# A scan followed by a mixture of adapters on one core: ScalarE copies the transposed weights as 32-bit words, early filler matmuls are halved, and the written-out orders of all engines are replaced

## The chip, the cores and the metric

The kernel runs on one core of a Trainium2 chip. A core has five instruction streams that run side by side and meet only at semaphores: TensorE (PE, with its weight loads as PEld), VectorE (DVE), ScalarE (ACT), GpSimd (POOL) and SyncE (SP), which here only issues transfers between device memory and on-chip memory. The metric is the time of one execution on the device in microseconds (us), as the median of several runs. Before the change it is 201.59 us (three runs, 201.13 to 202.28).

## What is computed

The inputs are `a` and `b`, each 8 x 6400 x 128 in float32. For each of the 8 sequences a linear recurrence runs along the 6400 steps, for 128 channels by themselves. Its 51200 rows x then go through eight small adapters of rank 16, of which each row takes the two with the highest gate logits:

```
h = a[:, t] * h + b[:, t];  x[:, t] = h          # the scan, 6400 steps
logits = x @ w_gate                              # 51200 x 8
top two of the 8 logits, softmax over the two -> weights w
out = x + sum over the two of  w * ((x @ A[e]) @ B[e])
```

## The kernel before

**Tiles.** The 51200 rows are cut into 100 chunks of 512 rows, 4 blocks of 128 rows each. Loads and stores take two chunks at a time (512 KB for `a`, 512 KB for `b`, 512 KB for the result); the first four chunks and the last four stores are single (256 KB). `NL = 6` buffers of two chunks hold each of `a` and `b`; the result waits in a ring of 72 blocks (18 chunks). Two chunks share a load so that the lower 64 partitions hold the first and the upper 64 the second.

**Stages of a chunk c**, with the names that the written-out orders use:

- `la`, `lb` (SP): loads. The very first `lb0` is issued by ACT, as are the three small weight loads `ca`, `cw`, `cb`.
- `A`, `B` (PE): transposes of `a` and `b` into PSUM, channels on partitions; `P{c}` does B of chunk c and A of chunk c+1 in alternation, 16 matmuls.
- `ae` (ACT): copy of the transposed `a` from PSUM to `a_st`, 128x512 float32.
- `sc` (DVE): the scan, 128x512, into the ring `xT` (float16). Each scan starts from the last column of the one before.
- `Z` (PE), `ze` (ACT): x times [A for all experts, gate] for a unit of 4 or 6 blocks, and its copy to `zl`.
- `g1` to `g8`, `gx` (DVE or POOL), `w1` (ACT, sigmoid): top-two gate for a group of usually 4 units, result `g`.
- `mu` (POOL or DVE): `zw = zl * g`, float16, 128x512.
- `T` (PE): four transposes of `zw` into PSUM (float16). `te` (DVE or ACT): copy of these 128x512 float16 values to `zwT`.
- `D` (PE): for each block, x again by an identity matmul, plus `zwT` times B, eight matmuls.
- `oe` (ACT or DVE): copy of the 128x512 float32 result to `outt`. `st` (SP): store. `st68` goes as two transfers of 124 and 4 partitions (`SPLIT`).
- `fi7` to `fi14` (PE): fillers, `FILL[c]` matmuls each on an identity, whose result is not read; `wu` are 16 more at the start. `sg` (ACT) is a sigmoid on a constant whose result is not read.

**What sets the order.** Nothing is decided while the kernel is built: the dictionary `ORDER` lists for each engine the names in the order of execution. Engines that can take an operation are named in `P.add` ("pool dve", "dve act"), and the list in which a name stands decides. `Program.waits` then puts semaphore waits in front of each operation. Every engine works its list in order, so an operation that waits holds up all behind it; SP waits in the same way in front of each load (until the buffer was read by its A, B or P) and each store (until its `oe` are done). All of SP's transfers enter one queue that 16 DMA engines work off.

The copies that the change touches are made by one helper and one operation:

```python
def copy(e, dst, src):
    return e.copy(dst, src) if e is eng["act"] else e.tensor_copy(dst, src)
...
o_te[c] = P.add("dve act", f"te{c}", J, [o_T[c]] + get(o_D, c - NW),
                lambda e: copy(e, zt, ptile[:, 0:C]))
```

`zt` is `zwT` of the chunk, `bank` the chunk's PSUM bank of 512 float32 columns and `ptile` the same bank seen as float16; J is 4, C is 512.

Of the kernel before, what the change touches and what calls it, by code (L numbers as in the profile page):

```python
# [16 lines left out]
FILL = {k: 4 for k in range(7, 15)}  # L17
# [6 lines left out]
NW = 4  # L24
NG = 8
NS = 16
TAIL_CHUNKS = 12
ORDER = {
# [16 lines left out]
    ),  # L45
    "act": (
# [16 lines left out]
    ),  # L63
    "dve": (
# [14 lines left out]
    ),  # L79
    "pool": (  # L80
# [8 lines left out]
    ),  # L89
# [9 lines left out]
    ),  # L99
# [81 lines left out]
def bass_associative_scan_2x2__then__mixture_of_adapters_kernel(  # L181
# [56 lines left out]
    with ExitStack() as stack:  # L238
# [125 lines left out]
        def get(d, k):  # L364
            return [d[k]] if k in d else []
# [365 lines left out]
```

## Time and profile before

| | before |
|---|---|
| median of three runs | 201.59 us (201.13 to 202.28) |
| the profiled execution, timed | 201.01 us |
| its span, first to last instruction on the core | 199.2 us |
| granted TensorE clock, mean | 0.994 |
| moved by DMA | 79.26 MB, mean 398 GB/s |
| PE / DVE / ACT / POOL busy | 185.2 / 175.0 / 176.9 / 136.0 us |

The profile page gives busy time by engine, the span in 40 slices, the DMA queues, the chain of work that ended last, and the costliest groups of instructions. Further views show the same execution by stretches of time, by groups of equal shape, as a timeline of one engine, and for the transfers of one tile the time from issue to landing. A group's row reads: line, engine, operation, output and inputs, shapes, count; then busy time and mean nanoseconds of one; then idle time of the engine just before and what ended it. A row of a stretch gives the busy microseconds of each engine with the count of its instructions, the granted clock, the mean busy share of the 16 DMA engines and GB/s. "L300" is line 300 of the kernel before.

### The profile page before, as it was taken

How to read it: one execution, taken by the hardware profiler on the slowest of the kernel's cores; microseconds unless marked ns; L12 is line 12 of the kernel's file. 1: busy time of each engine (PE TensorE's matmuls, PEld its weight loads, DVE VectorE, ACT ScalarE, POOL GpSimd, SP SyncE). 2: the span in 40 equal slices, each digit the busy share in tenths (PEclk: the TensorE clock that was granted, in tenths of full speed). 3: DMA queues.
4: the chain of work that ended last, by engine and by line, in shares of the span. 5: the costliest groups of instructions: out<-in, count | busy, mean ns of one | idle time of the engine just before them, and what ended most of it. 6: DMA issues, size and time to landing. Idle time of an engine off the chain costs nothing.

```text
span 199.2 us, 7709 instructions
## 1 busy us (share of the span) xinstructions
PE 185.2 (93%) x3224; PEld 165.5 (83%) x3224; DVE 175.0 (88%) x291; ACT 176.9 (89%) x327; POOL 136.0 (68%) x168
## 2 busy tenths in 40 slices
PE   6899999999998979999999999999999999999990
PEld 6778888889987968899989989889988978878970
DVE  1599999989999879799999999999999899899980
ACT  2378699999988979899999999999999989999981
POOL 3210186878786657969989998796598978676520
PEclk9999999999999999999999999999999999999997
DMA  5999999999999999999999999999999999999796
GB/s 214 385 414 406 410 407 407 409 406 410 411 410 413 414 411 412 415 414 408 414 415 406 411 410 416 411 411 415 414 412 414 417 410 412 406 393 392 298 405 254
DMA packets 22921, 79.26 MB, mean 398 GB/s; under 512 B 2664, under 2 KB 2920, under 8 KB 22888
## 3 DMA queue, kind: packets, MB, share of 16 engines
q1 hardware_dynamic: 22312, 78.39, 98.1%
q8 instruction: 25, 0.41, 0.8%
q10 hardware_dynamic: 576, 0.40, 0.6%
q14 instruction: 8, 0.07, 0.1%
HBM read 52.56 MB, written 26.21 MB: 395 GB/s over the span
## 4 chain that ended last, share of the span: by engine, by line
PE 80%; ACT 5%; DMA 4%; issue 3%; SPq 2%; POOL 2%; DVE 1%; DVEq 0%
PE pB L417 23%; PE pO L588 13%; PE pZ L500 13%; PE pO L578 12%; PE pO L589 10%; PE pA L417 5%; DMA a_tm<-in_a_dram 4%; ACT outt L300 3%; PE pA L446 2%; SPq L396 2%; POOL zw L569 2%; ACT zwT L300 1%; ACT a_st L435 1%; ACT zl L506 1%; DVE xT L482 1%
## 5 line engine op out<-in xcount | busy, mean ns | idle before, releaser
L482 DVE TENSOR_TENSOR_SCAN xT<-a_st,xT,pB 128x512 f16<-128x512 f32 x96 | 120.4, 1254 | 6.6 <-PE pA L417 3.1
L569 POOL TENSOR_TENSOR zw<-zl,g 128x512 f16<-128x512 f32 x90 | 94.5, 1065 | 29.2 <-DVE g L554 23.2
L417 PE MATMUL pB<-ident_f,b_tm 64*128 64x64 f32 (+1 forms) x784 | 67.5, 229 | 1.2 <-issue 0.5
L417 PE MATMUL pA<-ident_f,a_tm 64*128 64x64 f32 (+1 forms) x784 | 67.8, 229 | 0.6 <-issue 0.4
L435 ACT COPY a_st<-pA 128x512 f32<-128x512 f32 x100 | 59.0, 613 | 7.9 <-PE pA L417 7.2
L417 PEld LDWEIGHTS pB<-ident_f,b_tm 64*128 64x128 f32 (+1 forms) x784 | 55.8, 139 | 10.9 <-issue 3.4
L506 ACT COPY zl<-pZ 128x816 f32<-128x816 f32 (+1 forms) x69 | 58.1, 842 | 1.7 <-PE pZ L500 1.6
L588 PE MATMUL pO<-ident_h,xT 128*128 128x128 f16 x368 | 55.2, 233 | 2.0 <-issue 1.8
L417 PEld LDWEIGHTS pA<-ident_f,a_tm 64*128 64x128 f32 (+1 forms) x784 | 56.0, 139 | 1.2 <-DMA a_tm<-in_a_dram 0.7
L300 ACT COPY outt<-pO 128x512 f32<-128x512 f32 x87 | 52.2, 609 | 4.6 <-PE pO L589 4.1
L589 PE MATMUL pO<-cst_h,zwT 128*128 128x128 f16 x368 | 53.0, 219 | 1.7 <-issue 1.7
L588 PEld LDWEIGHTS pO<-ident_h,xT 128*128 128x128 f16 x368 | 46.3, 144 | 4.9 <-issue 2.1
L589 PEld LDWEIGHTS pO<-cst_h,zwT 128*128 128x128 f16 x368 | 39.6, 108 | 1.8 <-issue 1.8
L500 PE MATMUL pZ<-cst_h,xT 128*128 128x136 f16 x400 | 37.8, 229 | 0.5 <-issue 0.4
L578 PE MATMUL pO<-ident_h,zw 128*128 128x128 f16 x368 | 35.5, 220 | 1.1 <-POOL zw L569 0.4
L500 PEld LDWEIGHTS pZ<-cst_h,xT 128*128 128x128 f16 x400 | 30.6, 145 | 1.5 <-DVE cst_h L324 0.2
L578 PEld LDWEIGHTS pO<-ident_h,zw 128*128 128x128 f16 x368 | 22.3, 97 | 5.5 <-POOL zw L569 1.3
L300 DVE COPY zwT<-pO 128x512 f16<-128x512 f16 x56 | 23.0, 414 | 3.5 <-PE pO L578 3.1
L300 ACT COPY zwT<-pO 128x512 f16<-128x512 f16 x36 | 21.4, 600 | 0.9 <-PE pO L578 0.8
L545 POOL TENSOR_TENSOR L<-L,k 128x192 f32<-128x192 f32 x14 | 8.8, 631 | 4.6 <-DVE L L543 4.0
L482 DVE TENSOR_TENSOR_SCAN xT<-a_st,pB 128x512 f16<-128x512 f32 (+1 forms) x8 | 7.5, 938 | 4.5 <-PE pB L417 4.4
L548 POOL TENSOR_TENSOR k<-k,L 128x192 f32<-128x192 f32 (+1 forms) x17 | 9.1, 535 | 2.5 <-DVE L L539 1.8
(56 smaller groups left out, 120.0 us busy)
## 6 DMA issues: line engine op xcount, KB each, us to landing
a_tm<-in_a_dram SPq DMA_DIRECT2D x48, 512.0 KB, 13.3
b_tm<-in_b_dram SPq DMA_DIRECT2D x48, 512.0 KB, 13.4
out_dram<-outt SPq DMA_DIRECT2D x47, 512.0 KB, 11.9
a_tm<-in_a_dram SPq DMA_DIRECT2D x4, 256.0 KB, 4.9
out_dram<-outt SPq DMA_DIRECT2D x4, 256.0 KB, 4.0
b_tm<-in_b_dram SPq DMA_DIRECT2D x3, 256.0 KB, 5.6
out_dram<-outt SPq DMA_DIRECT2D x1, 496.0 KB
b_tm<-in_b_dram ACTq DMA_DIRECT2D x1, 256.0 KB, 4.0
```

Of the source, the lines that this page charges most:

```text
L300: return e.copy(dst, src) if e is eng["act"] else e.tensor_copy(dst, src)
L417: last = e.transpose(*args)
L435: lambda e: e.copy(a_st[c % NA][:, :], pA[:, c % 2, :]))
L482: last = e.tensor_tensor_scan(out=x[:, s0:s1], data0=a_st[c % NA][:, s0:s1], data1=pB[:, c % 2, s0:s1], initial=init, op0=ALU.mult, op1=AL ...
L500: last = e.matmul(pZ[:, k // (n // 2), o : o + W], xblock(b0 + k), Awg_h)
L506: lambda e: e.copy(zl[:, zb : zb + n, :].rearrange("p (h k) w -> p h (k w)", h=2), pZ[:, :, 0 : n // 2 * W]))
L545: d3 = wide(5, [d3], lambda e: e.tensor_tensor(out=ll, in0=ll, in1=kk, op=ALU.add))
L548: d6 = wide(7, [d2, d5], lambda e: e.tensor_tensor(out=kk, in0=kk, in1=ll, op=ALU.add))
L569: lambda e: e.tensor_tensor(out=wv, in0=zv, in1=gv, op=ALU.mult))
L578: last = e.transpose(ptile[:, k * 128 : k * 128 + 128], zz[:, k, :], ident_h[:, :])
L588: e.matmul(dst, xblock(b0 + k), ident_h[:, :], start=True, stop=False)
L589: last = e.matmul(dst, zt[:, k * 128 : k * 128 + 128], B_h, start=False, stop=True)
```

## The change

Three things are different in the program that runs.

1. `te` on ACT reads the PSUM bank as 256 float32 words and writes 256 words, in place of 512 float16 values. On DVE it stays as it was. (`J // 2` in the call is a number kept with the operation; it reaches no instruction.)
2. `FILL` is 2 in place of 4, so the eight fillers issue 16 matmuls in place of 32.
3. All five lists of `ORDER` are new. The set of names is the same. Places and store pairs (`STORES`, `SPLIT`, `NX`, `NO` and the like) are the same. Counted over the lists, operations change engine and place as follows:

| operation | before | after |
|---|---|---|
| `te` on ACT / DVE | 38 / 62 | 65 / 35 |
| `oe` on ACT / DVE | 95 / 5 | 86 / 14 |
| `mu` on POOL / DVE | 90 / 10 | 82 / 18 |
| `g2`, `g3`, `g6`, `g7` on POOL | 56 | 48 |
| ahead of `sc95` in DVE's list: `te` / `oe` / `mu` | 49 / 4 / 2 | 28 / 12 / 8 |
| ahead of `sc95` in DVE's list: `g2`, `g3`, `g5`, `g6`, `g7` together | 12 | 21 |
| ahead of `ae95` in ACT's list: `te` / `oe` | 29 / 72 | 50 / 64 |
| from `ae98` to the end of ACT's list: `te` / `oe` / `w1` | 7 / 18 / 6 | 11 / 15 / 5 |
| stores ahead of `lb98` in SP's list | 34 | 32 |

On DVE the first gate operations, `gx_0` and `g2_0`, stood between `sc3` and `sc4`; now they stand behind `sc5`. `AHEAD = 1000`, `TREE = ()` and `MASK = ()` are new names. With these values the slice that `AHEAD` takes of SP's list is empty and the branch on `MASK` is never taken, so they add no wait and no instruction.

```diff
-FILL = {k: 4 for k in range(7, 15)}
+FILL = {k:2 for k in range(7,15)}
+AHEAD = 1000
+TREE = ()
+MASK = ()
...
     "pe": (
-        "wu0 wu1 wu2 wu3 wu4 wu5 wu6 wu7 wu8 wu9 wu10 wu11 A0 wu12 wu13 wu14 wu15 B0 A1 B1 cm B2 A2 B3 A3 A4 Z0 P4 Z1 "
...
+        "wu0 wu1 wu2 wu3 wu4 wu5 wu6 wu7 wu8 wu9 wu10 wu11 A0 wu12 wu13 wu14 wu15 B0 A1 B1 A2 cm A3 B2 B3 A4 Z0 P4 Z1 "
...
     "act": (
-        "ca lb0 cb sg cw ae0 ae1 cc ae2 ae3 ae4 ze0 ze1 ae5 ae6 ze2 w1_0 ae7 ze3 ae8 ze4 ae9 te0 ae10 ae11 w1_1 ze5 "
...
-        "ae96 ae97 ze63 oe79 te80 te81 ze64 oe80 oe81 ae98 w1_16 te83 oe82 ze65 oe83 ae99 te85 oe84 ze66 oe85 w1_17 "
-        "te86 te87 ze67 oe86 oe87 te90 te89 oe91 w1_18 oe88 oe90 oe89 ze68 w1_19 oe92 oe93 w1_20 oe95 oe94 w1_21 te97 "
-        "oe96 oe97 oe98 oe99 "
+        "cw ca lb0 cb ae1 ae0 ae2 cc ae3 sg ae4 ze0 ae5 ze1 ae6 ze2 ae7 ze3 ae8 w1_0 ze4 ae9 ae10 ze5 te0 w1_1 ae11 "
...
+        "ae92 te74 te75 ae93 oe74 ze60 w1_15 ae94 ze61 ae95 ae96 oe76 oe77 te78 ze62 oe78 oe79 ze63 ae97 te81 oe80 "
+        "ze64 te82 oe81 w1_16 te83 oe82 ae98 oe83 ze65 te85 oe84 w1_17 oe85 te86 ae99 ze66 oe86 te90 oe87 te91 te88 "
+        "oe90 w1_18 te89 oe88 w1_19 ze67 te92 oe89 te93 ze68 te95 oe92 w1_20 te96 oe95 oe94 oe96 w1_21 te98 oe97 oe98 "
+        "oe99 "
...
     "sp": (
-        "la0 lb1 la1 la3 lb2 la2 lb3 la4 lb4 la6 lb6 la8 lb8 la10 lb10 la12 lb12 la14 lb14 la16 lb16 la18 lb20 lb18 "
...
-        "la84 st46 lb84 st48 la86 la88 lb86 lb88 st50 la90 st52 lb90 st54 la92 lb92 la94 st56 lb94 la96 st58 lb96 "
-        "st60 la98 st62 st72 st64 lb98 st66 st68 st78 st76 st70 st74 st82 st80 st86 st84 st90 st88 st92 st94 st96 "
+        "la1 la0 lb1 la2 lb2 la3 lb3 la4 lb4 la6 lb6 la8 lb8 la10 lb10 la12 lb12 la14 lb14 la16 lb16 la18 lb18 la20 "
...
+        "lb82 la84 lb84 la86 lb86 st48 la88 lb88 st50 la90 st52 lb90 la92 st54 lb92 st56 la94 lb94 la96 st58 st60 "
+        "lb96 st62 la98 lb98 st64 st70 st66 st72 st68 st80 st74 st76 st78 st82 st84 st86 st88 st90 st92 st94 st96 "
         "st97 st98 st99 "
...
+        for before, op in zip(self.order["sp"], self.order["sp"][AHEAD:]):
+            op.deps = op.deps + [before]
...
-            o_te[c] = P.add("dve act", f"te{c}", J, [o_T[c]] + get(o_D, c - NW),
-                            lambda e: copy(e, zt, ptile[:, 0:C]))
+            o_te[c] = P.add("dve act", f"te{c}", J // 2, [o_T[c]] + get(o_D, c - NW),
+                            lambda e: e.copy(zt.bitcast(F32), bank[:, 0 : C // 2]) if e is eng["act"]
+                            else e.tensor_copy(zt, ptile[:, 0:C]))
```

In the program that is built, ACT now loads an activation table twice: once ahead of its first copy (`ae1`) and once ahead of `sg`, which has moved from before `ae0` to between `ae3` and `ae4`. Before, it is loaded once, ahead of `sg`.

More of the change, by code (lines that the diff above doesn't have):

```diff
@@ L552, in gating @@
                     zlast[zpos[u] + k] = d5 if top else d2
-            o_g[gi] = wide(8, [a1, d5] + (get(o_mu, glast[gi - NG]) if gi >= NG else []),
-                           lambda e: e.scalar_tensor_tensor(
-                               out=gg, in0=ll, scalar=0.0, in1=sg, op0=ALU.is_ge, op1=ALU.mult))
+            free = get(o_mu, glast[gi - NG]) if gi >= NG else []
+            if gi in MASK:
+                d8 = wide(9, [d5, d6], lambda e: e.tensor_scalar(
+                    out=ll, in0=ll, scalar1=0.0, scalar2=1.0, op0=ALU.is_ge, op1=ALU.mult))
+                o_g[gi] = P.add("pool dve", f"gf_{gi}", nb, [a1, d8] + free,
+                                lambda e: e.tensor_tensor(out=gg, in0=ll, in1=sg, op=ALU.mult))
+            else:
+                o_g[gi] = wide(8, [a1, d5] + free, lambda e: e.scalar_tensor_tensor(
+                    out=gg, in0=ll, scalar=0.0, in1=sg, op0=ALU.is_ge, op1=ALU.mult))
         def back(gi, c):
```

103 rows, old and new, of the table ORDER are left out of this document.

## The prediction

> **What bounds the kernel now.** I read the page first (busy time, queues, chain), then the span by stretches, then when the last stores land.
>
> ```profile
> span 199.2 us, 7709 instructions
> PE 185.2 (93%) x3224; PEld 165.5 (83%) x3224; DVE 175.0 (88%) x291; ACT 176.9 (89%) x327; POOL 136.0 (68%) x168
> q1 hardware_dynamic: 22312, 78.39, 98.1%
> q8 instruction: 25, 0.41, 0.8%
> PE 80%; ACT 5%; DMA 4%; issue 3%; SPq 2%; POOL 2%; DVE 1%; DVEq 0%
> ```
>
> By this page four things are near their limit. The chain names PE and the ACT copies, but a chain follows what came last at each step and does not say how much slack stood beside it. The stretches give the DMA side (last two columns: mean busy share of the 16 engines, GB/s).
>
> ```profile
> 0.00:5.00 5.00, 3.33 (x16) 3.33 (x17) 0.56 (x2) 1.49 (x2) 1.67 (x8) 1.00 0.58 214
> 15.00:170.00 155.00, 149.44 (x2761) 134.48 (x2759) 145.03 (x207) 146.33 (x267) 118.92 (x144) 1.00 1.03 411
> 185.00:190.00 5.00, 4.90 (x80) 4.55 (x78) 4.82 (x25) 5.00 (x13) 3.07 (x5) 1.00 0.78 311
> 190.00:195.00 5.00, 4.00 (x60) 3.24 (x57) 3.28 (x14) 4.14 (x10) 0.47 (x1) 1.00 1.02 404
> 195.00:199.20 4.20, 0.00 (x0) 0.00 (x0) 0.00 (x0) 0.00 (x0) 0.00 (x0) 0.73 0.60 230
> ```
>
> For 155 us the transfers run at share 1.03 and 411 GB/s: full. At 411 GB/s the queue's 78.39 MB alone take 190.7 us, and the change leaves every byte in place. What is not full is the first 5 us (0.58) and 185 to 190 (0.78, 0.22 x 5 = 1.1 us). Is that last dip a hole in the chain of stores, which a faster tail would close? The landings tell. Four looks at SP's issues, the first that of a first load into an empty queue, then the stores `st86`, `st88`, and `st98` with `st99`:
>
> ```profile
> L396 SPq DMA_DIRECT2D a_tm<-in_a_dram x1: 382/382/382, 0.7 to 0.7; - x1
> DMA to landing us min/median/max: 3.1/3.1/3.1
> ...
> L631 SPq DMA_DIRECT2D out_dram<-outt x1: 332/332/332, 185.2 to 185.2; - x1
> DMA to landing us min/median/max: 4.7/4.7/4.7
> ...
> L631 SPq DMA_DIRECT2D out_dram<-outt x1: 492/492/492, 188.5 to 188.5; - x1
> DMA to landing us min/median/max: 5.2/5.2/5.2
> ...
> L631 SPq DMA_DIRECT2D out_dram<-outt x2: 518/574/630, 194.3 to 194.9; - x2
> DMA to landing us min/median/max: 3.9/3.9/3.9
> ```
>
> `st86` lands at 185.2 + 4.7 = 189.9, `st88`, three 512 KB stores on, at 193.7, the last store, four such units on (two whole, four halves), at 194.9 + 3.9 = 198.8. That is 1.27 us a unit in both stretches, and 524,288 bytes at 411 GB/s are 1.28 us. So the landings run at the full pace straight through the dip and to the end. I read it thus: a store has landed when its latest engine is done; the 16 have drifted apart (each of the 25 instruction fetches takes 0.8% x 16 x 199.2 / 25 = 1.0 us of a single engine, an estimate from the q8 row), the ones ahead ran dry in the dip, and the one furthest behind never did. It sets the end.
>
> The Trainium skill, "DMA: Bandwidth & Descriptors" (section "Why a DMA increments its semaphore by 16 and not by 1"), says that a transfer's engines finish independently and that only the full count means landed. The even landings beside a share of 0.78 agree with it; by it no copy engine can buy time below the slowest queue.
>
> How much later may compute be before that chain tears? An empty queue lands 256 KB in 3.1 us, the last store took 3.9: 0.8 us of slack. A 512 KB store would need 3.1 + 0.64 = 3.7 (half a unit more); `st86` had 1.0 to spare, `st88` 1.5. Within 0.8 us compute is covered; past it the end moves one for one.
>
> **The change, part by part.** The rows for the prices:
>
> ```profile
> L482 DVE TENSOR_TENSOR_SCAN xT<-a_st,xT,pB 128x512 f16<-128x512 f32 x92 | 117.4, 1276 | 6.2 <-PE pA L417 2.8 <-ACT a_st L435 1.6
> L569 POOL TENSOR_TENSOR zw<-zl,g 128x512 f16<-128x512 f32 x90 | 94.5, 1065 | 29.2 <-DVE g L554 23.2 <-PE pO L578 5.1 <-PE pA L578 0.6
> L435 ACT COPY a_st<-pA 128x512 f32<-128x512 f32 x100 | 59.0, 613 | 7.9 <-PE pA L417 7.2
> L506 ACT COPY zl<-pZ 128x816 f32<-128x816 f32 x62 | 53.7, 867 | 1.1 <-PE pZ L500 1.0
> L300 ACT COPY outt<-pO 128x512 f32<-128x512 f32 x87 | 52.2, 609 | 4.6 <-PE pO L589 4.1
> L300 DVE COPY zwT<-pO 128x512 f16<-128x512 f16 x56 | 23.0, 414 | 3.5 <-PE pO L578 3.1
> L300 ACT COPY zwT<-pO 128x512 f16<-128x512 f16 x36 | 21.4, 600 | 0.9 <-PE pO L578 0.8
> L569 DVE TENSOR_TENSOR zw<-zl,g 128x512 f16<-128x512 f32 x10 | 6.8, 684 | 0.0
> L446 PE MATMUL pA<-ident_f 128*128 128x128 f32 x32 | 5.0, 279 | 0.0
> L300 DVE COPY outt<-pO 128x512 f32<-128x512 f32 x5 | 3.4, 674 | 0.5 <-PE pO L589 0.5
> L317 ACT ACT_TABLE_LOAD x1 | 1.3, 1283 | 2.1 <-issue 2.1
> L549 ACT ACTIVATE sd<-k 128x32 f32<-128x32 f32 x5 | 1.2, 241 | 0.0
> L542 DVE TENSOR_TENSOR k<-zl,m 128x192 f32<-128x192 f32 x3 | 1.1, 353 | 0.0
> L357 ACT CAST cst_h<-pZ 128x128 f16<-128x128 f32 x1 | 0.3, 265 | 0.3 <-PE pZ L351 0.3
> ```
>
> *The word copy.* No row shows 256 words from PSUM. 512 elements cost 600 ns in float16 and 613 in float32, so the count decides and not the bytes. Between 128 and 512 elements the rows rise by (613 - 265) / 384 = 0.91 ns an element, between 512 and 816 by 0.84: 381 or 399 ns for 256. I take 0.39 us. The ends are 0.27 (128 elements) and 0.60 (no gain).
>
> *Sums over the kernel.* ACT: `te` 65 x 0.39 - 38 x 0.600 = +2.6, `oe` -9 x 0.609 = -5.5, together -2.9. DVE: `te` -27 x 0.414 = -11.2, `oe` 9 x 0.674 = +6.1, `mu` 8 x 0.684 = +5.5, eight gate operations x 0.353 = +2.8, together +3.2. POOL: -8 x 1.065 = -8.5 and the gate operations. So ACT's gain has been spent to free POOL, and DVE becomes the busiest of the copying engines.
>
> *Ahead of the tail.* Counted ahead of `sc95`, DVE gets -21 x 0.414 + 8 x 0.674 + 6 x 0.684 + 9 x 0.353 = +4.0 us; ACT, ahead of `ae95`, 50 x 0.39 - 29 x 0.600 - 8 x 0.609 = -2.8.
>
> ```profile
> 6.60:169.70 163.10, 156.63 (x2840) 140.03 (x2839) 151.96 (x218) 150.88 (x275) 119.28 (x145) 1.00 1.03 412
> ```
>
> From the first scan to `sc95` (169.7) DVE is idle 163.1 - 152.0 = 11.1 us, ACT 12.2. To keep pace DVE must do with 7.1 idle and ACT may have 15. DVE's waits there are mostly for PE and ACT (6.2 us on the scan rows); ACT is eased, and POOL's 23.2 us of waiting for `g` shrink. I take +0, between -2 (waits shrink by as much as ACT is eased) and +4.0 (none does).
>
> *Tail.* From `ae98` on ACT has 11 x 0.39 - 7 x 0.600 - 3 x 0.609 - 0.24 (one `w1`) = -2.0 us; DVE behind `sc95` about -0.5 (six `te` less, one `oe` and two `mu` more). The last `oe` comes some 1 to 2 us sooner after `sc97`. Its worth is nothing: the queue lands at 1.27 us a unit in any case. This cover is the 13 to 16 units still queued; if it were gone, the 2 us would show.
>
> *SP.* `lb98` stands behind two stores fewer and lands 2 x 1.28 = 2.6 us sooner; the bytes behind it are as many more. `st80` now stands in front of `st74`, `st76`, `st78` and waits for `oe81`; behind it are 13 units, 16.5 us, so it must start by 198.8 - 16.5 = 182.3 and be issued 2.5 us (3.1 - 0.64) ahead, by 179.8.
>
> ```profile
> 175.74 1.10 ACT L300 COPY outt<-pO 128x512 f32<-128x512 f32 x2
> ...
> 193.67 1.17 ACT L300 COPY outt<-pB 128x512 f32<-128x512 f32 x2 [0.23 <-PE pB L589]
> ```
>
> The first row is `oe80` and `oe81`, done at 176.8: 3 us to spare. The second is the last pair, done at 194.8. `la1` ahead of `la0` delays `A0` by half a unit, 0.6 us; the queue starts as early and is as full. Nothing.
>
> *Fillers.* 16 matmuls less are 2.5 us of PE between 14 and 26 us, where loads set the pace (share 1.03). Nothing; the clock column is 1.00 in every stretch, also where no filler runs.
>
> *Second table load.* 1.28 us, with the sigmoid 1.5, now stands between `ae3` and `ae4`.
>
> ```profile
> 11.65 0.59 ACT L435 COPY a_st<-pA 128x512 f32<-128x512 f32 x1 [0.32 <-PE pA L417]
> ...
> 13.40 2.64 DVE L482 TENSOR_TENSOR_SCAN xT<-a_st,xT,pB 128x512 f16<-128x512 f32 x2
> ```
>
> `ae4` ended 1.16 us before `sc4` began, so `sc4` comes up to 0.3 us later, less the two gate operations that no longer precede it. Nothing at the end, for the loads behind it are queued. Against this change speaks the Trainium skill, "ScalarE: Activation LUTs" (section "What ACT_TABLE_LOAD costs"), which puts a switch of tables at 1283 ns and a drain of 1380 on top; by the page `sc4` would come 1.7 us later, and if the loads did not cover it the time would be 203.2. The row agrees with the 1283; the drain no row here shows.
>
> **Sum.** 0 on the transfer chain: span 199.2, timed 201.0 as the profiled execution (1.8 us around its span). The median of the runs is 0.6 above that execution; I keep the distance and take 0.1 off for the slack in the tail: 201.5 us. What a measurement here can tell from no change is about 0.5%, 1.0 us.
>
> **Rivals.**
> - *Compute sets the end (faster).* For it: the chain, and the 1.1 us of idle DMA time at 185 to 190. Against it: the landings at 1.27 us a unit. It would give between 1.1 (the dip closed) and 2.0 us (ACT's tail): 199.6 to 200.5, say 200.1.
> - *DVE becomes the bound (slower).* Place: the stretch up to `sc95`. Price: +4.0, less 0.5 in its own tail and 0.8 of slack: +2.7, 204.3. It decides once DVE's idle time there stays above some 9 us (7.1, and 0.8 of slack and 1.0 of tolerance more). For it: DVE is the only engine given work in the stretch. Against: ACT and POOL, for which it waited, are eased.
> - *The word copy is no shorter (the change does not do what it says).* ACT would get 65 x 0.60 - 38 x 0.60 - 5.5 = +10.7 against 12.2 us idle: past the slack, some 204 to 208. Against: the 265 ns row.
> - *`st80` holds up SP* if `oe81` comes after 179.8, 3 us later than now; one for one beyond.
> - *The table switch costs its drain and the loads do not cover it:* 203.2.
>
> **Numbers.** No change 0.58 (201.5, own range 200.6 to 202.6). Compute sets the end 0.21. DVE the bound 0.11, word copy 0.04, `st80` 0.04, table 0.02: 0.21 slower. The range reaches to 200.0 (below it half of the faster case's reach) and to 203.4, which leaves out the upper part of the DVE case and the word copy, together under 2 in 10.
>
> **What would show it.** Right: last store landing at 1.27 us a unit; 1.03 and 411 GB/s in the middle; `te` on ACT near 390 ns; DVE near 178 us busy, ACT near 174, POOL near 123; the last `oe` at or before 194.8 without the span following it. Wrong: a store that lands 3.1 to 3.7 us after issue with all engines idle before it, or a share under 1 between 30 and 170 us, would put the end on compute; a bigger or smaller drift of the latest DMA engine would move the end with no copy involved.

## The result, and the profile after

The kernel after takes 202.45 us (median of 20 runs, 201.28 to 204.44), the kernel before 201.38 in the runs beside it (20 runs, 200.81 to 203.83). The ratio is 1.0047, 95% interval 1.0028 to 1.0066: half a per cent slower, where no change was forecast. The medians are over all executions; the ratio leaves out those in a slower state. The profiled execution of after is one of its quickest, 201.36 us timed and 199.6 us long, so only 0.4 us of the difference can be seen in its trace; that the scatter of the start, below, accounts for the rest is an estimate.

From the page of the kernel after: span, busy time, the transfer queue, the chain that ended last, and the word copies of `te` on ScalarE.

```profile
span 199.6 us, 7685 instructions
...
PE 185.4 (93%) x3208; PEld 164.5 (82%) x3208; DVE 178.2 (89%) x289; ACT 174.3 (87%) x346; POOL 125.1 (63%) x152
...
q1 hardware_dynamic: 22312, 78.39, 98.1%
...
PE 47%; ACT 19%; DVE 16%; DMA 6%; issue 4%; POOL 3%; SPq 3%; DVEq 0%
...
L594 ACT COPY zwT<-pO 128x256 f32<-128x256 f32 x59 | 22.6, 398 | 3.4 <-PE pO L589 2.8
```

The bytes are the same, and the engines stand where the sums put them (DVE 178, ACT 174). The chain has turned from PE 80% to a mixture. The prediction did not trust that view, and no reading here rests on it.

Stretches of the kernel after (columns as before: PE, PEld, DVE, ACT, POOL, clock, share of the DMA engines, GB/s):

```profile
8.40:171.90 163.50, 156.37 (x2817) 138.59 (x2818) 155.86 (x221) 149.69 (x291) 109.81 (x130) 1.00 1.03 412
15.00:170.00 155.00, 149.19 (x2715) 132.41 (x2715) 147.76 (x212) 142.48 (x279) 109.01 (x130) 1.00 1.03 412
175.00:180.00 5.00, 5.00 (x97) 4.49 (x95) 4.88 (x14) 4.76 (x11) 1.67 (x2) 1.00 0.75 299
185.00:190.00 5.00, 5.00 (x86) 4.92 (x84) 5.00 (x23) 5.00 (x16) 3.04 (x3) 1.00 0.87 343
190.00:195.00 5.00, 4.62 (x70) 3.91 (x68) 4.25 (x20) 4.67 (x13) 2.13 (x4) 1.00 0.90 360
```

The first row runs from the first scan to `sc95`, as 6.60 to 169.70 did before: 163.5 us in place of 163.1. DVE has 155.9 busy in place of 152.0, and its idle time falls from 11.1 to 7.6. So the 4 us of added work were absorbed but for 0.4 us. But the stretch begins 1.8 us later, and `sc95` comes 2.2 us later. In the middle the queue is as full as before (1.03, 412). New is the dip at 175 to 180; before, that stretch had 1.02.

Why the stretch begins later, from the timelines of the opening. Before (first column the start, second the duration, in brackets the wait ahead):

```profile
5.38 0.58 ACT L435 COPY a_st<-pA 128x512 f32<-128x512 f32 x1 [1.74 <-PE pA L417]
...
6.60 1.22 DVE L482 TENSOR_TENSOR_SCAN xT<-a_st,pB 128x512 f16<-128x512 f32 x1 [4.39 <-PE pB L417]
```

After:

```profile
2.62 1.28 ACT L440 ACT_TABLE_LOAD   x1 [2.62 <-issue]
7.29 1.07 ACT L440 COPY a_st<-pA 128x512 f32<-128x512 f32 x2 [3.39 <-PE pA L422]
...
10.67 1.28 ACT L322 ACT_TABLE_LOAD   x1
11.96 0.21 ACT L322 ACTIVATE warm<-ident_f 128x8 f32<-128x8 f32 x1
...
8.40 1.22 DVE L487 TENSOR_TENSOR_SCAN xT<-a_st,pB 128x512 f16<-128x512 f32 x1 [6.18 <-ACT a_st L440]
9.72 6.89 DVE L487 TENSOR_TENSOR_SCAN xT<-a_st,xT,pB 128x512 f16<-128x512 f32 x5
```

The first scan needs `ae0` and `B0`. Before, it waited for `B0`. After, it waits for ScalarE: the two copies that start at 7.29 are `ae1` and then `ae0`. In ScalarE's list `ae1` now stands first; it needs `A1`, which in PE's list stands behind `B0`, which needs `lb0`, which has gone from second to third on ScalarE's queue. So `ae0`, which needed only `A0`, waits for all of that. The issue of `lb0` and its time to landing, before and after:

```profile
L396 ACTq DMA_DIRECT2D b_tm<-in_b_dram x1: 451/451/451, 1.2 to 1.2; - x1
DMA to landing us min/median/max: 4.0/4.0/4.0
...
L401 ACTq DMA_DIRECT2D b_tm<-in_b_dram x1: 453/453/453, 1.7 to 1.7; - x1
DMA to landing us min/median/max: 4.4/4.4/4.4
```

It lands at 6.1 in place of 5.2. The last row of the timeline after shows five scans back to back: the second table load, inside that stretch, held up no scan.

And the end of the kernel after, the last copy on ScalarE and the last two stores:

```profile
195.94 0.59 ACT L305 COPY outt<-pB 128x512 f32<-128x512 f32 x1 [0.91 <-PE pB L601]
...
L643 SPq DMA_DIRECT2D out_dram<-outt x2: 332/512/693, 195.3 to 196.6; - x2
...
DMA to landing us min/median/max: 2.5/2.5/2.5
```

The last `oe` is done at 196.5 (before 194.8), and the last store lands 2.5 us after its issue where it took 3.9. By the 16 landing counts of `st99` in the trace, all its DMA engines finish within 0.2 us of each other (198.90 to 199.09), where before they lay 1.1 us apart (197.64 to 198.74). Before, the engine furthest behind set the end; in this execution of after, the last copy does. When the queue alone would have been done with the new orders is not shown here: in open_act, below, its latest engine ends at 199.4.

### The profile page after: what moved, and what is told of

It is laid out like the page before. It is cut to its first block, busy times and chain, and to the rows that moved or that the text cites. A ratio compares the mean times of both kernels' runs of the same rounds, so it can differ in the third digit from the quotient of the medians.

```text
span 199.6 us, 7685 instructions
## 1 busy us (share of the span) xinstructions
PE 185.4 (93%) x3208; PEld 164.5 (82%) x3208; DVE 178.2 (89%) x289; ACT 174.3 (87%) x346; POOL 125.1 (63%) x152
## 4 chain that ended last, share of the span: by engine, by line
PE 47%; ACT 19%; DVE 16%; DMA 6%; issue 4%; POOL 3%; SPq 3%; DVEq 0%
PE pB L422 12%; DVE xT L487 11%; PE pO L600 9%; PE pZ L505 7%; PE pO L589 7%; DMA a_tm<-in_a_dram 6%; ACT zl L511 6%; PE pO L601 6%; ACT outt L305 5%; ACT a_st L440 5%; SPq L401 3%; PE pA L422 3%; POOL zw L580 2%; ACT zwT L594 2%; DVE zwT L595 2%
## 5 line engine op out<-in xcount | busy, mean ns | idle before, releaser
L580 POOL TENSOR_TENSOR zw<-zl,g 128x512 f16<-128x512 f32 x82 | 87.8, 1088 | 25.3 <-DVE g L565 17.7
L601 PE MATMUL pO<-cst_h,zwT 128*128 128x128 f16 x368 | 52.4, 219 | 0.7 <-issue 0.7
L305 ACT COPY outt<-pO 128x512 f32<-128x512 f32 x80 | 47.3, 602 | 5.4 <-PE pO L601 4.8
L589 PE MATMUL pO<-ident_h,zw 128*128 128x128 f16 x368 | 34.1, 220 | 2.4 <-ACT outt L305 1.4
L594 ACT COPY zwT<-pO 128x256 f32<-128x256 f32 x59 | 22.6, 398 | 3.4 <-PE pO L589 2.8
L547 POOL TENSOR_TENSOR k<-zl,m 128x192 f32<-128x192 f32 (+1 forms) x11 | 5.9, 534 | 15.8 <-DVE m L546 15.8
L595 DVE COPY zwT<-pO 128x512 f16<-128x512 f16 x33 | 13.5, 411 | 1.1 <-PE pO L589 0.9
L550 POOL TENSOR_TENSOR L<-L,k 128x192 f32<-128x192 f32 (+2 forms) x14 | 7.9, 565 | 8.2 <-DVE L L548 7.7
```

What stands on the lines that cost most here:

```text
L580: lambda e: e.tensor_tensor(out=wv, in0=zv, in1=gv, op=ALU.mult))
L589: last = e.transpose(ptile[:, k * 128 : k * 128 + 128], zz[:, k, :], ident_h[:, :])
L594: lambda e: e.copy(zt.bitcast(F32), bank[:, 0 : C // 2]) if e is eng["act"]
L595: else e.tensor_copy(zt, ptile[:, 0:C]))
L601: last = e.matmul(dst, zt[:, k * 128 : k * 128 + 128], B_h, start=False, stop=True)
```

## The experiments

In the table, first scan is its start, `sc95` and last `oe` their ends in the one profiled execution, landing the last engine's end of `st99`. The ratio is to the kernel before on the same chip, over 6 to 20 runs.

| kernel | first scan | `sc95` | last `oe` | landing | ratio (95%) |
|---|---|---|---|---|---|
| before | 6.6 | 171.0 | 194.8 | 198.7 | 1 |
| after | 8.4 | 173.2 | 196.5 | 199.1 | 1.0047 (1.0028 to 1.0066) |
| words_only | 6.7 | 170.2 | 194.2 | 198.7 | 0.9985 (0.9962 to 1.0007) |
| no_words | 9.6 | 179.5 | 205.1 | 207.2 | 1.0381 (1.0350 to 1.0411) |
| old_start | 7.0 | 172.5 | 196.2 | 199.2 | 1.0000 (0.9981 to 1.0020) |
| oe_to_act | 9.2 | 176.3 | 199.1 | 201.7 | 1.0134 (1.0104 to 1.0163) |
| open_act | 7.0 | 172.1 | 195.4 | 199.4 | 1.0006 (0.9991 to 1.0021) |
| open_sp | 9.2 | 173.9 | 196.8 | 199.8 | 1.0046 (1.0019 to 1.0072) |
| ae0_first | 7.9 | 172.7 | 196.9 | 200.2 | 1.0022 (0.9998 to 1.0046) |
| ae1_alone | 9.2 | 173.9 | 196.7 | 199.3 | 1.0037 (1.0006 to 1.0068) |
| late_table | 8.1 | 174.7 | 198.1 | 200.7 | 1.0009 (0.9985 to 1.0033) |

**The word copy by itself, and the new orders without it.** `words_only` is the kernel before with the new `te`:

```diff
-            o_te[c] = P.add("dve act", f"te{c}", J, [o_T[c]] + get(o_D, c - NW),
-                            lambda e: copy(e, zt, ptile[:, 0:C]))
+            o_te[c] = P.add("dve act", f"te{c}", J // 2, [o_T[c]] + get(o_D, c - NW),
+                            lambda e: e.copy(zt.bitcast(F32), bank[:, 0 : C // 2]) if e is eng["act"]
+                            else e.tensor_copy(zt, ptile[:, 0:C]))
```

> The kernel before with the word copy alone (38 copies on ACT as words; orders and fillers of before). It takes 38 x 0.2 = 7.7 us off ACT. If the transfers set the end of the kernel before (my theory, with 0.8 us of slack for compute), the time stays within 0.3% of before, 0.995 to 1.002, and the stores still land at 1.27 us a unit. If compute sets the end (rival), ACT's tail shortens by 7 copies x 0.2 = 1.4 us and the time falls to about 0.993 or lower.

`no_words` is the kernel after with that edit undone.

> The changed kernel with the float16 copy in place of the word copy (its new orders and fillers stay). ACT gets 65 x 0.2 = 13 us more, where it has 12.5 us idle between 15 and 170 us. If lateness of compute past the slack is what costs the changed kernel its microsecond, this one is some 2 to 5 us slower still (ratio to before 1.015 to 1.03). If the cost came from the transfers (order of stores, drift of engines), the copy changes little: 1.003 to 1.008.

In the old orders the shorter copy is worth nothing that can be measured (0.9985): its last `oe` is 0.6 us sooner and the last store lands when it did. In the new orders it is worth 3.3% (1.0381 against 1.0047), more than the 1.015 to 1.03 expected: with 65 `te` on ScalarE the long copy makes compute the bound. Page and one stretch of no_words:

```profile
PE 189.7 (91%) x3208; PEld 165.6 (80%) x3208; DVE 180.3 (87%) x289; ACT 186.0 (90%) x346; POOL 124.6 (60%) x152
...
L305 ACT COPY zwT<-pO 128x512 f16<-128x512 f16 x59 | 35.9, 629 | 3.4 <-PE pO L589 3.0
...
170.00:185.00 15.00, 14.45 (x244) 12.69 (x242) 13.91 (x23) 14.64 (x28) 10.25 (x12) 1.00 0.63 253
```

ScalarE is busy 97.6% of that stretch and the transfers starve at a share of 0.63.

**The opening put back.** `old_start` is the kernel after with the opening of the kernel before on ScalarE and on SP:

```diff
     "act": (
-        "cw ca lb0 cb ae1 ae0 ae2 cc ae3 sg ae4 ..."
+        "ca lb0 cb sg cw ae0 ae1 cc ae2 ae3 ae4 ..."
     "sp": (
-        "la1 la0 lb1 la2 lb2 la3 lb3 ..."
+        "la0 lb1 la1 la3 lb2 la2 lb3 ..."
```

> The changed kernel with the opening of before on ACT (ca lb0 cb sg cw ae0 ae1 cc ae2 ae3) and SP (la0 lb1 la1 la3 lb2 la2). In the changed kernel the first scan starts 1.8 us later (8.4 against 6.6), because ae0 now stands behind ae1. Theory start: that lateness is carried to the end by a full DVE; with the old opening the last oe comes 1.0 to 1.8 us earlier and the time is that of before, 0.998 to 1.002. Theory load: the scans had caught up by chunk 10 and DVE's added work is what is late; the time stays at 1.004 to 1.006.

The whole loss is gone: 1.0000. All other orders, the moved work on DVE, the place of `st80` and the halved fillers are still those of after. So none of them costs anything that can be measured. `old_start` even keeps the dip:

```profile
175.00:180.00 5.00, 5.00 (x95) 4.53 (x95) 4.87 (x14) 4.76 (x12) 1.86 (x3) 1.00 0.78 312
```

In that dip SP stands before `st80` until `oe81` is done, and the time does not move for it. In after, the row of SP's longest wait from 160 us on (total, times, longest), and the copy `oe81` with the operation behind it on ScalarE, are:

```profile
SPq L643 <- ACT sd L554: 10.4, 1, 10.4
...
178.36 0.62 ACT L305 COPY outt<-pO 128x512 f32<-128x512 f32 x1
178.93 0.36 ACT L554 ACTIVATE sd<-k 128x192 f32<-128x192 f32 x1
```

The first row names `sd`, the sigmoid `w1_16` right behind `oe81` in ScalarE's list; the store itself needs the copy, which is done at 179.0.

**DVE relieved.** In `oe_to_act` nine `oe` ahead of `sc95` go from DVE to ScalarE, each to the place where its `D` is done:

```diff
     "dve": (
-        "... te7 sc25 oe7 g1_4 ... sc87 oe69 te71 ..."
+        "... te7 sc25 g1_4 ... sc87 te71 ..."
     "act": (
-        "... oe6 ze15 ae26 te8 ze16 ... ae88 ze57 oe68 ae89 te70 ..."
+        "... oe6 ze15 ae26 oe7 te8 ze16 ... ae88 ze57 oe68 oe69 ae89 te70 ..."
```

> The changed kernel with nine of the fourteen oe copies of DVE (7, 19, 41, 48, 53, 56, 61, 64, 69) given back to ACT, each behind the operations whose PE work comes earlier. DVE loses 9 x 0.674 = 6.1 us ahead of sc95, ACT gets 9 x 0.609 = 5.5. Theory load (DVE has become the bound): sc95 comes 1 to 2 us earlier and the time is that of before, 0.998 to 1.002. Theory start: no more than 0.2% better, 1.003 to 1.006.

Its stretch from the first scan to `sc95`:

```profile
9.15:175.06 165.91, 157.40 (x2822) 138.91 (x2822) 151.09 (x212) 153.52 (x301) 109.73 (x130) 1.00 1.03 412
```

DVE has 4.8 us less to do there than in after, and the stretch is 2.4 us longer; 1.0134 is worse than either theory named. Taking work off DVE did not bring `sc95` forward. ScalarE has 3.8 us more; whether its load or the places chosen for the nine copies made the stretch longer stays open.

**How far the transfers set the end.** `thin` keeps every transfer and PE's work and leaves out the work that its expectation names.

```diff
-            gating(gi)
-            o_mu[c] = P.add("pool dve", f"mu{c}", J, [o_ze[u] for u in us] + [o_g[gi]] + get(o_T, c - NW),
-                            lambda e: e.tensor_tensor(out=wv, in0=zv, in1=gv, op=ALU.mult))
...
-                    last = e.transpose(ptile[:, k * 128 : k * 128 + 128], zz[:, k, :], ident_h[:, :])
+                    last = e.transpose(ptile[:, k * 128 : k * 128 + 128], xblock(b0 + k), ident_h[:, :])
```

> The kernel before with the same transfers in the same order and the same PE program, but with the copies left out: no copy of Z, no gating, no mu, no te (T transposes x instead of the weighted product, and D adds x times B, so the output is x + x B and not the reference's). ACT keeps ae and oe, DVE the scans, POOL nothing. Theory transfers: with copies no longer near their limit the time falls by at most 0.5%, ratio 0.995 to 1.000, because the landings already run at the queue's pace to the end. Theory compute: without some 190 us of copying work the end comes well earlier, ratio 0.985 or lower.

```profile
PE 185.2 (93%) x3224; PEld 171.3 (86%) x3224; DVE 131.8 (66%) x113; ACT 111.3 (56%) x198; POOL 2.8 (1%) x8
```

With 43 us less on DVE, 66 on ScalarE and 133 on POOL the time falls by 0.4% (0.9959, 0.9941 to 0.9977). Its last store lands at 198.8, as before. Only this much is to be had from the copying engines in the kernel before.

`no_split` lets `st68` go as one store:

```diff
-SPLIT = {68: [124, 4]}
+SPLIT = {}
```

> The kernel before with st68 as one store of 128 partitions, not as 124 and 4. Theory of the prediction 'the DMA engine furthest behind sets the end, and the split keeps work from the ones behind': with every engine given an equal share of st68 the latest engine gets 32 KB more, +0.6 to +1.3 us, ratio 1.003 to 1.006. Rival 'the 16 even out by themselves': 0.999 to 1.001.

```profile
span 201.5 us, 7708 instructions
...
L631 SPq DMA_DIRECT2D out_dram<-outt x2: 333/333/333, 195.3 to 195.9; - x2
...
DMA to landing us min/median/max: 5.1/5.1/5.1
```

1.0057 (1.0037 to 1.0077), inside the forecast; the profiled execution is the slowest of the six. The last store is issued at 195.9, where late1 below issues it at 196.1 and loses nothing. Here it lands at 201.0, 5.1 us on: the same bytes, dealt out otherwise over the 16 engines, move the end with no copy involved.

**How much slack compute has.** `late1` and `late2` are the kernel before with one and two copies on ScalarE ahead of `oe91`, whose result is not used (about 0.95 us each expected, 1.05 measured):

```diff
     "act": (
-        "... te90 te89 oe91 w1_18 oe88 ..."
+        "... te90 te89 dl0 oe91 w1_18 oe88 ..."
+            o_dl.append(P.add("act", f"dl{k}", 0, [o_cm] + o_dl, lambda e: e.copy(
+                spread[:, :, :], ident_f[:, :].unsqueeze(1).broadcast_to([128, DL, 128]))))
```

> The kernel before with one more ScalarE copy (128x1024 float16 out of an identity, about 0.95 us, result not read) ahead of oe91, so that oe91 and all later stores' copies come about 0.95 us later. Slack theory: 0.8 us of it is covered, the time rises by 0 to 0.4 us, ratio 1.000 to 1.002. Without slack (compute sets the end) it rises by the full 0.95 us, ratio 1.0045 to 1.005.

> The kernel before with two copies of about 0.95 us each ahead of oe91 on ScalarE (their results are not used), so that the last stores are issued some 1.9 us later; one such copy left the time at 0.9987. Theory 'compute has about 0.8 to 1.2 us of slack to the transfers, and past it the end moves one for one': last oe at 196.5 to 197.0, +0.5 to +1.1 us, ratio 1.002 to 1.0055. Rival 'no bound, the end follows neither' : ratio 0.998 to 1.001. Rival 'compute sets the end and the one copy was hidden elsewhere': +1.9 us, 1.009.

The last stores of late1 and of late2, in this order:

```profile
L633 SPq DMA_DIRECT2D out_dram<-outt x2: 332/332/332, 195.5 to 196.1; - x2
...
DMA to landing us min/median/max: 2.6/2.6/2.6
```

```profile
L633 SPq DMA_DIRECT2D out_dram<-outt x2: 332/332/332, 196.5 to 197.1; - x2
...
DMA to landing us min/median/max: 2.4/2.4/2.4
```

`late1` issues its last store 1.2 us later than before and lands it at 196.1 + 2.6 = 198.7, as before: 0.9987. `late2` issues 2.2 us later and lands at 199.5, 0.75 later: 1.0025 (0.9997 to 1.0052), which alone would not exclude no change. Issued late, such a store lands in 2.4 to 2.5 us in late2 and after (2.0 in no_words), not in the 3.1 that the prediction took from a load. The slack of the kernel before is therefore about 3.9 - 2.5 = 1.4 us, and compute sets the end once the last store is issued after 198.7 - 2.5 = 196.2.

**Which part of the opening.** `open_act` puts back ScalarE's part alone, `open_sp` SP's alone (the lines of `old_start`'s diff, one each).

> The kernel after with ScalarE's opening alone as in the kernel before (sigmoid's table first, ae0 ahead of ae1, lb0 second on its queue); SP's opening stays that of after (la1 ahead of la0). Theory 'ScalarE's order makes the scan late': first scan near 7.0 to 7.4 us, ratio 1.000 to 1.001, as with both put back. Rival 'the order of the loads does': first scan at 8 us or later, ratio 1.003 to 1.005.

> The kernel after with SP's opening alone as in the kernel before (la0 lb1 la1 ...); ScalarE's opening stays that of after (ae1 ahead of ae0, tables loaded twice). Theory 'ScalarE's order': nothing is mended, first scan 8 to 9.5 us, ratio 1.003 to 1.006; it could be worse, since ae0 now stands behind ae1 while la1 comes third. Rival 'the order of the loads': ratio 1.000 to 1.002.

First scans of open_act and of open_sp:

```profile
7.02 1.22 DVE L484 TENSOR_TENSOR_SCAN xT<-a_st,pB 128x512 f16<-128x512 f32 x1 [4.79 <-PE pB L419]
```

```profile
9.18 1.22 DVE L484 TENSOR_TENSOR_SCAN xT<-a_st,pB 128x512 f16<-128x512 f32 x1 [6.95 <-ACT a_st L437]
```

1.0006 against 1.0046. ScalarE's opening carries the loss; `la1` ahead of `la0` carries none that can be measured. Then ScalarE's three moves apart, each against the opening of after:

```diff
     "act": (
         "cw ca lb0 cb ae1 ae0 ae2 cc ae3 sg ae4 ..."    (after)
+        "cw ca lb0 cb ae0 ae1 ae2 cc ae3 sg ae4 ..."    (ae0_first)
+        "ca lb0 cb sg cw ae1 ae0 cc ae2 ae3 ae4 ..."    (ae1_alone)
+        "ca lb0 cb cw ae0 ae1 ae2 cc ae3 sg ae4 ..."    (late_table)
```

> The changed kernel with ae0 ahead of ae1 in ACT's list and nothing else. In the changed kernel the first scan waited 6.2 to 7.4 us for a_st, since ae1 and with it A1, B0 and lb0 had to be done before ae0. If that one exchange is the cause, the first scan starts near 7.4 and most of the 0.47% goes: 1.000 to 1.002. If the cause is in the rest of the opening (lb0 issued third on ACT, la1 ahead of la0, the second table load between ae3 and ae4), it stays at 1.003 to 1.005.

> The kernel after with ScalarE's opening as in the kernel before but for ae1 ahead of ae0. B's first half is loaded early here, so A1 may come sooner than in after and the first scan waits less: first scan between 7.4 and 8.2 us. Theory 'the order of the two copies is half of the loss, the late load of B the other': 1.001 to 1.003. If the copies' order alone is the loss: 1.004 to 1.006; if it is nothing by itself: 1.000.

> The kernel after with ScalarE's opening as in the kernel before but for the sigmoid's table, which keeps its late place between ae3 and ae4 (so that the tables are loaded twice). The prediction priced the second load at nothing. If that holds: first scan near 7.0 us, 1.000 to 1.0015, as with all of ScalarE's opening put back. If the table is part of the loss: the scans wait for ae4 around 13 us, and 1.002 to 1.005.

`ae1` ahead of `ae0` by itself costs 0.37% (1.0006 to 1.0068), between its two theories, and its first scan waits for ScalarE until 9.22, later than forecast. With only that pair put right 1.0022 is left, with an interval that touches 1. `late_table` gives 1.0009, so nothing is shown against the second table load. The three intervals overlap: which move costs most in the median is not shown. The executions of ae1_alone lie between 201.0 and 203.7, those of open_act between 201.1 and 202.1; none of the long ones was profiled.

The traces say more of the first scan. With `lb0` second on ScalarE's queue it landed at 5.1 to 5.6 us (before, old_start, open_act, ae1_alone, late_table), with `lb0` third at 6.1 to 7.3 (after, no_words, oe_to_act, open_sp, ae0_first, words_late_open). With `ae1` first behind such a load, the first scan came 2.3 us after the landing each time (five traces, 8.40 to 9.58): `B0`, `A1` and two copies stand in between. With `ae0` first it came 0.8 us after it (ae0_first, 7.12 to 7.93). So the order of the two copies is worth 1.5 us there, and the late load the rest, which is also what scatters. Why `lb0`, issued 0.5 us later, lands up to 2 us later stays open.

A second source of scatter is TensorE's pace. The profiled execution of `late_table`, the slowest of its runs, missed the forecast of 7.0: the first scan began at 8.08, and its waits are for `B` and not for ScalarE:

```profile
8.08 1.22 DVE L484 TENSOR_TENSOR_SCAN xT<-a_st,pB 128x512 f16<-128x512 f32 x1 [5.86 <-PE pB L419]
9.77 1.28 DVE L484 TENSOR_TENSOR_SCAN xT<-a_st,xT,pB 128x512 f16<-128x512 f32 x1 [0.34 <-PE pB L419]
12.19 5.48 DVE L484 TENSOR_TENSOR_SCAN xT<-a_st,xT,pB 128x512 f16<-128x512 f32 x4 [1.15 <-PE pB L419]
```

The first loads were not late (`lb0` landed at 5.4, in open_act at 5.6). TensorE was: groups of four transposes in late_table, then one in open_act.

```profile
6.91 1.06 PE L419 MATMUL pB<-ident_f,b_tm 128*128 128x128 f32 x4
9.47 1.06 PE L419 MATMUL pA<-ident_f,a_tm 128*128 128x128 f32 x4
11.06 0.61 PE L419 MATMUL pA<-ident_f,a_tm 128*128 128x128 f32 x4
...
6.30 0.60 PE L419 MATMUL pB<-ident_f,b_tm 128*128 128x128 f32 x4
```

Up to about 10.9 us a group took 1.06 us in place of 0.60. The clock column reads 1.00 for these stretches; the trace's first clock record, of full speed, begins at 10.9 us, in open_act at 4.8. In ae1_alone the groups take over 1.0 us up to 7.5, so part of its 9.22 is this and not the order.

**The same opening in the old orders.** `words_late_open` is words_only with the opening of after on ScalarE and SP. TensorE's and DVE's openings stay those of before.

> The kernel before with the word copy and with the changed kernel's opening on ACT (cw ca lb0 cb ae1 ae0 ae2 cc ae3 sg ae4) and SP (la1 la0 lb1 la2 lb2 la3 lb3); the rest of the orders is that of before. It starts its scans 1.8 to 3 us late as the changed kernel does, but DVE has 11 us idle behind it in place of 7.6, and ACT 7.7 us less work. If the lateness is carried only because DVE is full (theory carry), it is absorbed here: 0.997 to 1.001. If a late first scan costs whatever follows (for example through the loads), 1.003 to 1.005.

It loses 2.06% (1.0166 to 1.0245), four times as much as the opening costs in the new orders and more than either theory named. So DVE's idle time did not absorb it. But this does not settle why after loses: TensorE's list of before has `A2` behind `cm` and `B2`, so that `ae2` begins at 11.86 where it began at 9.18 in after, and the granted clock falls here, as it does not in after. Four stretches of it, then the first two of words_only:

```profile
5.00:15.00 10.00, 7.09 (x71) 5.95 (x69) 5.13 (x6) 3.56 (x6) 1.67 (x1) 1.00 1.03 393
15.00:20.00 5.00, 3.71 (x42) 2.96 (x40) 3.40 (x10) 3.71 (x9) 0.75 (x3) 0.66 1.03 410
20.00:30.00 10.00, 10.00 (x169) 8.58 (x166) 9.12 (x14) 7.25 (x13) 1.81 (x3) 1.00 1.03 406
30.00:40.00 10.00, 9.88 (x181) 8.73 (x182) 9.49 (x12) 9.54 (x19) 7.36 (x10) 1.00 0.79 292
```

```profile
5.00:15.00 10.00, 9.40 (x104) 7.77 (x104) 7.58 (x13) 5.75 (x11) 1.52 (x3) 1.00 1.04 403
15.00:20.00 5.00, 5.00 (x92) 4.39 (x88) 4.91 (x9) 3.83 (x8) 0.30 (x1) 1.00 1.03 407
```

PE works 7.1 of 10 us in place of 9.4. Then the granted clock is 0.66 over the next 5 us, PE does 42 matmuls in place of 92, and at 30 to 40 us the queue runs short for the first time (share 0.79, 292 GB/s). The last `oe` is 4.1 us later than in words_only (198.4), and the latest DMA engine ends at 202.8, 1.6 us behind the first. How much of the 4 us the late start, the mismatch of the lists and the clock make was not taken apart.

## Why the prediction was wrong

*What held.* The word copy: 0.39 us taken, 0.398 measured. The sums: DVE 178, ACT 174, POOL 125 for "near 123". The middle: 1.03 and 412 GB/s. That the transfers set the end of the kernel before, through the engine furthest behind: `thin` and `words_only` leave the end within 0.4%, `no_split` moves it by 0.57% with the same copies. DVE's added 4.0 us: taken as +0, and the stretch grew by 0.4 in after, by 0.7 in open_act and 1.1 in old_start. Fillers, `st80` and the second table load at nothing: `old_start` has the first two and 1.0000, `late_table` the third and 1.0009. Of `st80` the limit was close: `oe81` had to be done by 179.8, was done at 179.0. Of the table's drain, which the Trainium skill, "ScalarE: Activation LUTs" (section "What ACT_TABLE_LOAD costs"), puts on top of 1283 ns, the trace shows none: the copy ahead of it ends at 10.65, the load begins at 10.67 and takes 1.28, and the activation begins at 11.96. One reading was off without effect: "the clock column is 1.00 in every stretch" overlooks the last row shown, 0.73 from 195 us on, where TensorE has no work left.

*The step that failed* is the opening: "`la1` ahead of `la0` delays `A0` by half a unit, 0.6 us ... Nothing." It priced SP's list, which costs nothing, and left out ScalarE's, where the diff puts `ae1` ahead of `ae0` and `lb0` third. Walked through, the lists gave the answer: `ae0` behind `ae1`, `A1` behind `B0`, `B0` behind `lb0`. Its price was 1.8 us of first scan in the profiled execution, and 2.5 to 3.0 in five others with `ae1` first (`no_words`, `oe_to_act`, `open_sp`, `ae1_alone`, `words_late_open`: 9.15 to 9.58). With ScalarE's part alone put back the time is 1.0006.

*The tail* came nearly as forecast: "The last `oe` comes some 1 to 2 us sooner after `sc97`." From the end of `sc97` to the last `oe` it is 15.3 us in place of 16.2, 0.9 sooner. What failed is "the last `oe` at or before 194.8": `sc97` itself ends 2.6 us later (181.3 for 178.7), 1.8 from the start, 0.4 from the stretch to `sc95` and 0.4 between `sc95` and `sc97`. So the last `oe` comes 1.7 us later. Even with ScalarE's old opening it comes 0.6 later (open_act), with both openings 1.4 (old_start).

*The second miss* is the slack, mis-sized as 0.8 where the runs give about 1.4. It was on the safe side, and it fits the new orders with the old opening coming out at 1.0000: their last `oe` at 195.4 to 196.2 lies just inside.

Together: +1.7 - 1.4 = +0.3 us for the profiled execution, where the landing moved by 0.35 and the timed execution by 0.35. A single trace does not carry so small a difference: old_start, whose runs show no loss, lands at 199.2 in its own. By the ratio after is 0.95 us slower (0.47% of 201.4). What makes the rest is not shown. The five other starts came 0.75 to 1.2 us later than after's own, and if the end followed them in full, 0.3 would become 1.1 to 1.5 (an estimate); but ae1_alone, 0.8 later, lands 0.2 later than after, and open_sp, also 0.8 later, lands 0.7 later. In short, that ScalarE's opening costs the half per cent is shown by the exchange; that it does so by going past a slack which the new orders had half spent is argued from these traces.

*The rivals.* "Compute sets the end" came true in the wrong direction: in the profiled execution of after the last copy sets it, later than before. "DVE the bound" fell by its own condition (idle 7.6, under the 9 named) and by `old_start`, which keeps all of DVE's work and takes 1.0000. "Word copy no shorter" would have been dearer than its price of 204 to 208: `no_words` took 209.17.

## What to carry to other kernels

When orders written by hand are replaced, follow the first results through every engine's list, each operation with all that stands ahead of it, before adding up busy time: a swapped pair and a load one place later at the start cost more here than 4 us of work moved in the middle. An engine that is hidden behind the transfers has a finite slack; measure it by adding a known delay, and take the landing time on an empty queue from a transfer of the same kind. And a saving is worth what the orders around it need: the same copy was worth nothing in one set of orders and 3.3% in another.

## What the runs showed of the hardware

The granted clock can fall without a long pause of TensorE. After 5 to 15 us with PE at 7.1 of 10 us it was 0.66 over the next 5 us in `words_late_open`. The busy share alone does not decide it: oe_to_act, with the same 7.1, kept 1.00.

```profile
5.00:15.00 10.00, 7.14 (x83) 5.97 (x82) 5.45 (x6) 5.69 (x11) 1.67 (x1) 1.00 1.03 393
15.00:20.00 5.00, 4.75 (x86) 3.90 (x82) 4.90 (x10) 4.14 (x8) 1.19 (x4) 1.00 1.02 405
```

The Trainium skill, "TensorE: Matmul & The Clock Gate" (Part 1, "What's actually happening"), has the clock halved after an idle window of some 3.4 us; here PE was short of work for longer than that, but its longest single wait between 5 and 15 us was 1.6 us, and the one right before the fall 1.3 us (to 16.4):

```profile
PE pB L414 <- DVE ident_h L315: 1.6, 1, 1.6
```

So the trace agrees with the halving (the granted clock was 0.5 from 16.6 to 20.0 us, which makes (1.6 + 0.5 x 3.4) / 5 = 0.66), and shows that no single gap of that length is needed. What sets it off here stays open.

TensorE's faster pace does not begin at a fixed time: four transposes took 1.06 us up to 10.9 us in `late_table` and 0.60 us from 5.9 us on in `open_act`, though PE worked without a wait over 0.2 us in both from 5.4 us to then.

How bytes fall on the 16 DMA engines is worth half a per cent: without `SPLIT`, which cuts one store into 124 and 4 partitions, the ratio is 1.0057.
